# The first weight block of a fused attention and MLP kernel, in two parts, with two layer-1 items interleaved

## The chip, the cores and the metric

The kernel runs on one core of one Trainium2 chip. The metric is the device time of one execution in microseconds (us). Several executions of a kernel are timed and the median is given; one more execution is recorded by the hardware profiler.

## The reference

Causal attention with a decay bias, over 8 batches of 8 heads, 576 positions and a head size of 64, and then a two-layer MLP with exact GELU over the 4608 tokens. `w_in` is 512 x 2048, `w_out` is 2048 x 512, all in float32.

```python
scores = scale * np.matmul(q, k.transpose(0, 1, 3, 2))
cum = np.cumsum(np.maximum(s, 0.0), axis=-1)
bias = -(cum[:, :, :, None] - cum[:, :, None, :])
scores = np.where(causal, -1000000000.0, scores + np.minimum(bias, 0.0))
attn = softmax(scores)                       # rows divided by their sum + 1e-09
x = (attn @ v).transpose(0, 2, 1, 3).reshape(B * S, H * D)
h = x @ w_in
out = (0.5 * h * (1.0 + erf(h / sqrt(2)))) @ w_out
```

## The kernel before

The order of instructions on every engine is written out by hand (a manual schedule). The work has two interleaved streams: attention for a batch of 576 tokens, and the MLP for a chunk of 512 tokens. While chunk `c` goes through the MLP, attention for batch `c + 1` is done between its matmuls. Ahead of the loop stands attention for batch 0 alone.

Attention writes its output, transposed, into `xT`, a ring of 1536 token columns with four rows of blocks (`NP` = 4, 128 values each). For one batch, `av_main(b, 0, ...)` writes rows 0 and 1 for its first 512 tokens, and `av_main(b, 1, ...)` rows 2 and 3. Each consists of the matmuls `av_d` and `av_o` (L459), two pairs of ScalarE activations that form the reciprocal (L474, L475), and four VectorE products into `xT` (L499). The last 64 tokens of a batch are the tails: `av_tails(b, slot)` does 48 small matmuls into one PSUM bank (`av_t`, L459), the reciprocal, and one product (L520). Chunk 0 is tokens 0 to 511, so it does not read batch 0's tails; chunk 1 does.

Layer 1 of a chunk has eight items. An item (`l1_item(c, f2, k0, k1)`, L536) takes 256 columns of `w_in` and consists of 8 matmuls (L546), each over 512 tokens: for each of two groups of 128 columns, one for each of the four rows of `xT`. With `k0, k1 = 0, 2` it does its first half only, the 4 matmuls over rows 0 and 1, and with `k0 = 2` its second half, those over rows 2 and 3. Then one GELU activation (L552, for the last item two at L555) reads the item's two PSUM banks. The pairs of banks are called X, Y and Z, single banks M[0] and M[1]; `order[c]` says in which turn the items of a chunk take X, Y and Z, and later code takes its banks from the same tuple. Layer 2 (`l2_item`, L570, in chunks 0 and 1) multiplies the result with `w_out`.

The weights are loaded by transfers that GpSimd issues (`nc.gpsimd.dma_start`). They stand in its queue behind `behind_v(0, 1)`, a copy that waits for a part of `v` of batch 0. `load_w(0, i)` (L257, L260) loads 1024 columns of `w_in` in four transfers, one for each group of 32 partitions, and changes float32 to bf16 on the way; `load_w(1, i)` (L271) loads a quarter of `w_out` in one. The queue holds them in this order: 8 transfers of `w_in`, 2 of `w_out`, the 4 loads of `q` and `k` for batch 1 (`load_front`, L106), 2 more of `w_out`. Later, SyncE's `behind(1, ...)` (L144) waits for a part of `w_out` and then issues the loads of `v` for batch 1 (`raw_v`, L225), which VectorE scales into `vv` (`scale_v`, L247). VectorE also forms sums of `w_out` (`sums_b`, L598). `squares_v` (L237) is a pass of ScalarE over `raw_v`.

Chunk 0's order on TensorE was: 4 matmuls of item 0 over rows 0 and 1, the tails of batch 0 in bank X, 4 matmuls of item 0 over rows 2 and 3, then items 1 to 7. Chunk 1 already has the other order: first halves of items 0 and 1, tails in M[0], second halves of both.

Of the kernel before, what the change touches and what calls it, by code (L numbers as in the profile page):

```python
# [19 lines left out]
def kernel(  # L20
# [10 lines left out]
    nc = tc.nc  # L31
# [17 lines left out]
    dff = moe_w_in.shape[1]  # L49
    KO = (H * D) // 128  # L50
# [44 lines left out]
    X, Y, Z = "xyz"  # L95
    M = ("m0", "m1")
# [53 lines left out]
    def behind_v(b, st):  # L150

        nc.gpsimd.tensor_copy(seen_v[:, b : b + 1], raws[b, "v"][0:1, st, 0, 0:1])
# [3 lines left out]
    w_in_r = const.tile([128, KO, dff], bf16, name="w_in_r")  # L156
    w_out_r = const.tile([128, FT, KO * 128], fp16, name="w_out_r")
# [84 lines left out]
    def scale_v(b, sts, eng, h0=0, h1=H):  # L242
        t = raws[b, "v"]
        vb = vv[b % 2]
        for st0, st1 in sts:
            n_st = 128 if st1 < ST else SL
            eng.tensor_tensor(  # L247
                vb[:n_st, st0:st1, h0:h1, :],
                t[:n_st, st0:st1, h0:h1, :],
                wb[:n_st, st0:st1, b * H + h0 : b * H + h1]  # L250
                .unsqueeze(3).to_broadcast([n_st, st1 - st0, h1 - h0, D]),
                op=MULT,
            )

    STS = [(st, st + 1) for st in range(ST)]

    def load_w(which, i):  # L257
        if which == 0:
            for g in range(4):
                nc.gpsimd.dma_start(  # L260
                    out=w_in_r[g * 32 : g * 32 + 32, :, i * 1024 : (i + 1) * 1024],
                    in_=bass.AP(
                        tensor=moe_w_in.tensor,
                        offset=moe_w_in.offset + g * 128 * dff + i * 1024,
                        ap=[[dff, 32], [32 * dff, KO], [1, 1024]],
                    ),
                )
        else:
            src = moe_w_out.rearrange("(fo p) m -> p fo m", p=128)[:, i * 4 : (i + 1) * 4, :]
            dst = w_out_r[:, i * 4 : (i + 1) * 4, :]  # L270
            nc.gpsimd.dma_start(out=dst, in_=src)  # L271


    cum, s_pos = s_two
# [147 lines left out]
    def sc_mm(b, p, slots, u0=0):  # L422
        if u0 == 0:
            P_of[b, p] = work.tile([128, 2, PW], bf16, tag="P", bufs=4, name="P")
        P = P_of[b, p]
        for u, slot in enumerate(slots, u0):
            s_ps = bank(slot, [128, 2, 512], fp32, "sc_ps")
            for jt, i0, n, off in UNITS[u]:
                for e in range(2):
                    nc.tensor.matmul(  # L430
                        s_ps[:, e, off : off + n],
                        lhsT=qkT[b % 2][e * 64 : e * 64 + 64, 1, p, jt * 128 : jt * 128 + 128],
                        rhs=qkT[b % 2][e * 64 : e * 64 + 64, 0, p, i0 : i0 + n],
                        start=True, stop=True,
                    )
            nc.scalar.activation(  # L436
                P[:, :, UO[u] : UO[u] + UW[u]], s_ps[:, :, : UW[u]], func=AF.Exp, scale=scale
            )
# [70 lines left out]
    def tails_pe(b, slot):  # L509
        o = bank(slot, [128, 2, 3, SL], fp32, "av_t")  # L510
        for t in (None, 0, 1):
            for qd in range(2):
                av_mm(b, qd, o[:, qd, 0 if t is None else 1 + t], t, TAIL)
        return o

    def tails_out(b, o):
        ln = work.tile([128, 2, SL], fp32, tag="lnt", bufs=1, name="lnt")
        recip(ln, o[:, :, 0], 2)
        for lo, hi, x0 in ring(b, 512, SL):
            nc.vector.tensor_tensor(  # L520
                xT[:, :, x0 : x0 + hi - lo].rearrange("p (a t) x -> p a t x", t=2),
                o[:, :, 1:3, lo:hi],
                ln[:, :, lo:hi].unsqueeze(2).to_broadcast([128, 2, 2, hi - lo]), op=MULT,
            )

    def av_tails(b, slot):
        tails_out(b, tails_pe(b, slot))
# [3 lines left out]

    h_of, o_of = {}, {}

    order = {0: (Y, Z, X)}

    def l1_item(c, f2, k0=0, k1=None):  # L536
        k1 = KO if k1 is None else k1
        if f2 == 0 and k0 == 0:
            gT_of[c] = work.tile([128, FT, NB], fp16, tag="gT", bufs=1, name="gT")
        if k0 == 0:  # L540
            h_of[c, f2] = bank(order[c][f2 % 3], [128, 2, NB], fp32, "h_ps")
        h_ps = h_of[c, f2]
        for i in range(2):
            ft = f2 * 2 + i
            for ko in range(k0, k1):
                nc.tensor.matmul(  # L546
                    h_ps[:, i, :], lhsT=w_in_r[:, ko, ft * 128 : (ft + 1) * 128],
                    rhs=xT[:, ko, c * NB % XW : c * NB % XW + NB],
                    start=(ko == 0), stop=(ko == KO - 1),
                )  # L550
        if k1 == KO and f2 < FT // 2 - 1:
            nc.scalar.activation(gT_of[c][:, f2 * 2 : f2 * 2 + 2, :], h_ps, func=AF.Gelu)  # L552
        elif k1 == KO:
            for i in range(2):
                nc.scalar.activation(gT_of[c][:, f2 * 2 + i, :], h_ps[:, i], func=AF.Gelu)  # L555
# [174 lines left out]
    sc_mm(0, 2, (X, Y))  # L730
    sc_mm(0, 3, (Z, X))
    behind_v(0, 1)
    for i in range(2):
        load_w(0, i)
    for i in range(2):
        load_w(1, i)
    for qd in range(2):
        for n in "qk":
            load_front(1, n, qd)
    for i in range(2, 4):  # L740
        load_w(1, i)
    scale_v(0, STS[0:3], nc.vector)
    mask(0, 2, nc.vector)
    scale_v(0, STS[3:5], nc.vector)
# [3 lines left out]

    for c in range(NCH):
        nb = c + 1  # L750
        if c == 1:
            l1_item(c, 0, 0, KO - 2)
            l1_item(c, 1, 0, KO - 2)
            av_tails(1, M[0])
            l1_item(c, 0, KO - 2)
            l1_item(c, 1, KO - 2)
        else:
            l1_item(c, 0, 0, KO - 2)
            if c == 0:
                av_tails(0, X)  # L760
            l1_item(c, 0, KO - 2)
            l1_item(c, 1)
        if 1 < c and nb < B:
# [168 lines left out]
    with tc.If(rv > 0):  # L932
        with tc.tile_pool(name="gen", bufs=1) as gen, tc.tile_pool(
# [24 lines left out]
            with tc.For_i(0, B, 1) as b:  # L958
# [8 lines left out]
                for h in range(H):  # L967
                    cb = gen.tile([128, S], fp32, tag="cb", bufs=2, name="cb")
                    nc.sync.dma_start(
                        out=cb, in_=c_dram[bass.ds(b * H + h, 1), :].to_broadcast([128, S])  # L970
# [14 lines left out]
                    for it in range(ST):  # L985
# [41 lines left out]
                        g = (h // 2) * 32  # L1027
# [5 lines left out]
            with tc.For_i(0, NCH, 1) as c:  # L1033
                g = gen.tile([128, FT, NB], bf16, name="gg")
# [49 lines left out]
```

## Time and profile before

| | |
|---|---|
| Median of 3 runs | 321.77 us (321.12 to 322.37) |
| Profiled execution, its own time | 320.83 us |
| Span of the profiled execution | 319.0 us |
| TensorE busy | 298.6 us (94%) |
| ScalarE busy | 237.3 us (74%) |
| VectorE busy | 205.2 us (64%) |
| Layer 1 (L546), chain that ended last | 39% of the span |

Times in views of the trace are us from the start of the span. PE is TensorE's matmuls and PEld its weight loads, DVE is VectorE, ACT ScalarE, POOL GpSimd, SP SyncE. A line of the timeline gives start, duration, engine, source line, operation, output and inputs, count, and in brackets the idle time of the engine before it and what ended it. Granted clock (PEclk) is TensorE's clock as a share of full speed.

### The profile page before, as it was taken

How to read it: one execution, taken by the hardware profiler on the slowest of the kernel's cores; microseconds unless marked ns; L12 is line 12 of the kernel's file. 1: busy time of each engine (PE TensorE's matmuls, PEld its weight loads, DVE VectorE, ACT ScalarE, POOL GpSimd, SP SyncE). 2: the span in 40 equal slices, each digit the busy share in tenths (PEclk: the TensorE clock that was granted, in tenths of full speed). 3: DMA queues.
4: the chain of work that ended last, by engine and by line, in shares of the span. 5: the costliest groups of instructions: out<-in, count | busy, mean ns of one | idle time of the engine just before them, and what ended most of it. 6: DMA issues, size and time to landing. Idle time of an engine off the chain costs nothing.

```text
span 319.0 us, 8165 instructions
## 1 busy us (share of the span) xinstructions
PE 298.6 (94%) x3402; PEld 184.1 (58%) x3402; DVE 205.2 (64%) x405; ACT 237.3 (74%) x322; POOL 96.1 (30%) x176
## 2 busy tenths in 40 slices
PE   1769999899999999999999999999999999999991
PEld 0554444544454477647764776477647864784681
DVE  3786317967469758596877487748684875342550
ACT  3775687888965798889887988798779886666510
POOL 6554006205052283409440854076400000000000
PEclk9997999999999999999999999999999999999997
DMA  7999999985913595977699679948890030011003
GB/s 118 205 171 207 206 202 154 273 193 143 189 54 98 99 212 127 257 137 168 132 219 210 147 151 226 207 118 181 190 236 7 2 134 0 2 67 66 2 33 109
DMA packets 77388, 45.05 MB, mean 141 GB/s; under 512 B 63136, under 2 KB 69280, under 8 KB 77344
## 3 DMA queue, kind: packets, MB, share of 16 engines
q1 hardware_dynamic: 67136, 24.93, 33.9%
q0 software_dynamic: 10208, 19.53, 31.7%
q8 instruction: 28, 0.46, 0.6%
q14 instruction: 16, 0.13, 0.2%
HBM read 36.85 MB, written 9.44 MB: 145 GB/s over the span
## 4 chain that ended last, share of the span: by engine, by line
PE 83%; DMA 6%; ACT 5%; DVE 2%; issue 1%; POOL 1%; SPq 0%; ACTq 0%; POOLq 0%
PE h_ps L546 39%; PE o_al L618 16%; PE o_ga L618 8%; PE o_ps L570 5%; PE sc_ps L430 4%; PE o_be L618 4%; PE av_o L459 3%; DMA w_in_r<-in_moe_w_in_dram 3%; PE av_d L459 2%; DMA raw_v<-in_v_dram 2%; ACT junk L237 2%; DMA fq<-in_q_dram 2%; ACT P L436 2%; PE av_t L459 1%; DVE vv L247 1%
## 5 line engine op out<-in xcount | busy, mean ns | idle before, releaser
L546 PE MATMUL h_ps<-xT,w_in_r 128*128 128x512 bf16 x576 | 128.4, 382 | 2.5 <-DMA w_in_r<-in_moe_w_in_dram 2.0
L546 PEld LDWEIGHTS <-w_in_r 128*128 128x128 bf16 x576 | 56.1, 98 | 68.6 <-issue 4.6
L552 ACT ACTIVATE gT<-h_ps 128x1024 f16<-128x1024 f32 x63 | 62.9, 1019 | 26.7 <-PE h_ps L546 26.6
L436 ACT ACTIVATE P<-sc_ps 128x1024 bf16<-128x1024 f32 x64 | 60.3, 1030 | 3.4 <-PE sc_ps L430 3.3
L618 PEld LDWEIGHTS <-S 128*128 128x128 f16 x448 | 42.1, 98 | 6.7 <-issue 0.8
L229 DVE TENSOR_REDUCE amx<-qkT 128x2 f32<-128x1152 bf16 x32 | 41.5, 1344 | 0.1
L609 DVE TENSOR_TENSOR S<-gT 128x1024 f16<-128x1024 f16 x28 | 19.3, 688 | 31.2 <-ACT gT L555 24.0
L618 PEld LDWEIGHTS <-gT 128*128 128x128 f16 x336 | 32.0, 98 | 7.1 <-issue 1.8
L444 DVE TENSOR_TENSOR P<-P,tri_bf 128x512 bf16<-128x512 bf16 x64 | 25.9, 421 | 14.0 <-ACT P L436 13.5
L570 PE MATMUL o_ps<-w_out_r,gT 128*128 128x512 f16 x128 | 30.0, 380 | 0.0
L618 PE MATMUL o_al<-T,S 128*128 128x256 f16 x224 | 27.7, 273 | 0.0
L197 POOL DMA_DIRECT2D raw_k<-in_k_dram x25 | 21.0, 849 | 15.4 <-ACT junk L237 15.4
L430 PE MATMUL sc_ps<-qkT 64*128 64x256 bf16 (+2 forms) x320 | 22.2, 264 | 3.0 <-DVE qkT L400 1.7
L499 DVE TENSOR_TENSOR xT<-av_o,ln 128x256 bf16<-128x256 f32 (+2 forms) x72 | 23.7, 387 | 2.0 <-ACT ln L475 1.1
L247 DVE TENSOR_TENSOR vv<-raw_v,wb 128x512 bf16<-128x512 f32 (+2 forms) x25 | 23.7, 1001 | 0.0
L197 POOL DMA_DIRECT2D raw_q<-in_q_dram x25 | 21.1, 854 | 2.7 <-POOL seen_v L148 2.7
L430 PEld LDWEIGHTS <-qkT 64*128 64x128 bf16 x320 | 13.8, 98 | 12.7 <-issue 7.4
L400 DVE COPY qkT<-tr_ps 128x576 bf16<-128x576 bf16 (+1 forms) x15 | 12.0, 834 | 14.1 <-PE tr_ps L391 14.1
L237 ACT ACTIVATE junk<-raw_v 128x2048 bf16<-128x2048 f32 (+1 forms) x16 | 20.3, 1268 | 0.3
L570 PEld LDWEIGHTS <-gT 128*128 128x128 f16 x128 | 11.5, 98 | 13.6 <-issue 0.7
L475 ACT ACTIVATE ln<-ln,lnb 128x256 f32<-128x256 f32 x32 | 16.3, 508 | 1.0
L459 PEld LDWEIGHTS <-vv 128*32 128x32 bf16 x768 | 16.4, 102 | 0.9 <-issue 0.3
(114 smaller groups left out, 334.4 us busy)
## 6 DMA issues: line engine op xcount, KB each, us to landing
raw_v<-in_v_dram SPq DMA_DIRECT2D x32, 256.0 KB, 4.9
out_dram<-o_sb SPq DMA_DIRECT2D x12, 512.0 KB, 4.3
raw_q<-in_q_dram POOLq DMA_DIRECT2D x20, 256.0 KB, 4.6
raw_k<-in_k_dram POOLq DMA_DIRECT2D x20, 256.0 KB, 6.1
out_dram<-o_sb SPq DMA_DIRECT2D x11, 256.0 KB, 3.6
w_in_r<-in_moe_w_in_dram POOLq DMA_DIRECT2D x8, 256.0 KB, 8.7
w_out_r<-in_moe_w_out_dram POOLq DMA_DIRECT2D x4, 512.0 KB, 13.6
fq<-in_q_dram POOLq DMA_DIRECT2D x6, 288.0 KB, 6.1
```

The source lines that it names most:

```text
L197: nc.gpsimd.dma_start(out=t[:n_st, st], in_=src)
L229: nc.vector.tensor_reduce(amx[:, b * NP + p], qkT[b % 2][:, :, p, :S], axis=AX, op=ALU.max, apply_absolute_value=True)
L237: nc.scalar.activation(n[:n_st, : (st1 - st0) * H * D], t[:n_st, st0:st1].rearrange("p s h d -> p (s h d)"), func=AF.Square, accum_out=amv ...
L247: eng.tensor_tensor(vb[:n_st, st0:st1, h0:h1, :], t[:n_st, st0:st1, h0:h1, :], wb[:n_st, st0:st1, b * H + h0 : b * H + h1] .unsqueeze(3).t ...
L430: nc.tensor.matmul(s_ps[:, e, off : off + n], lhsT=qkT[b % 2][e * 64 : e * 64 + 64, 1, p, jt * 128 : jt * 128 + 128], rhs=qkT[b % 2][e * 6 ...
L436: nc.scalar.activation(P[:, :, UO[u] : UO[u] + UW[u]], s_ps[:, :, : UW[u]], func=AF.Exp, scale=scale)
L444: eng.tensor_tensor(d, d, tri_bf.unsqueeze(1).unsqueeze(1).to_broadcast([128, 2, 2, 128]), op=MULT)
L459: nc.tensor.matmul(o[g * 32 : g * 32 + 32, lo : lo + n], lhsT=(wb[:, jt, b * H + 2 * g + qd : b * H + 2 * g + qd + 1].to_broadcast([128, 3 ...
L546: nc.tensor.matmul(h_ps[:, i, :], lhsT=w_in_r[:, ko, ft * 128 : (ft + 1) * 128], rhs=xT[:, ko, c * NB % XW : c * NB % XW + NB], start=(ko ...
L552: nc.scalar.activation(gT_of[c][:, f2 * 2 : f2 * 2 + 2, :], h_ps, func=AF.Gelu)
L570: nc.tensor.matmul(o_ps, lhsT=gT[:, ft, sub * 128 : (sub + 1) * 128], rhs=w_out_r[:, ft], start=(ft == 0), stop=(ft == FT - 1),)
L618: nc.tensor.matmul(o[u], lhsT=lhs[:, f, u * 128 : u * 128 + 128], rhs=rhs[:, f], start=start and f == 0 and (by_sub or u == 0), stop=f == ...
```

## The change

The first 1024 columns of `w_in` are loaded as two blocks of 512 columns, each in four transfers; the second 1024 columns stay one block of four. That makes 12 transfers instead of 8. Items 0 and 1 read the first block, items 2 and 3 the second, items 4 to 7 the third. Chunk 0's layer 1 takes the order of chunk 1: the first halves of items 0 and 1, the tails in M[0], the second halves of items 0 and 1, then items 2 to 7. `order[0]` becomes X, Y, Z, so item 0 takes X, item 1 takes Y and item 2 takes Z; all later uses of the tuple shift with it.

```diff
-    def load_w(which, i):
-        if which == 0:
-            for g in range(4):
-                nc.gpsimd.dma_start(
-                    out=w_in_r[g * 32 : g * 32 + 32, :, i * 1024 : (i + 1) * 1024],
...
+    def load_w_in(m0, m1):
+        for g in range(4):
+            nc.gpsimd.dma_start(
+                out=w_in_r[g * 32 : g * 32 + 32, :, m0:m1],
+                in_=bass.AP(
+                    tensor=moe_w_in.tensor,
+                    offset=moe_w_in.offset + g * 128 * dff + m0,
+                    ap=[[dff, 32], [32 * dff, KO], [1, m1 - m0]],
+                ),
+            )
...
-    order = {0: (Y, Z, X)}
+    order = {0: (X, Y, Z)}
...
     behind_v(0, 1)
+    for m0, m1 in ((0, 512), (512, 1024), (1024, 2048)):
+        load_w_in(m0, m1)
     for i in range(2):
-        load_w(0, i)
-    for i in range(2):
-        load_w(1, i)
+        load_w_out(i)
...
-        if c == 1:
+        if c < 2:
             l1_item(c, 0, 0, KO - 2)
             l1_item(c, 1, 0, KO - 2)
-            av_tails(1, M[0])
+            av_tails(c, M[0])
             l1_item(c, 0, KO - 2)
             l1_item(c, 1, KO - 2)
         else:
             l1_item(c, 0, 0, KO - 2)
-            if c == 0:
-                av_tails(0, X)
             l1_item(c, 0, KO - 2)
             l1_item(c, 1)
```

More of the change, by code (lines that the diff above doesn't have):

```diff
@@ L255, with load_w_out @@
     STS = [(st, st + 1) for st in range(ST)]
-    def load_w(which, i):
-        if which == 0:
-            for g in range(4):
-                nc.gpsimd.dma_start(
-                    out=w_in_r[g * 32 : g * 32 + 32, :, i * 1024 : (i + 1) * 1024],
[L262 to L271, printed above, removed]
+    def load_w_in(m0, m1):
[8 more added lines that the diff above has]
+            )
+    def load_w_out(i):
+        src = moe_w_out.rearrange("(fo p) m -> p fo m", p=128)[:, i * 4 : (i + 1) * 4, :]
+        nc.gpsimd.dma_start(out=w_out_r[:, i * 4 : (i + 1) * 4, :], in_=src)
     cum, s_pos = s_two
@@ L740 @@
     for i in range(2, 4):
-        load_w(1, i)
+        load_w_out(i)
     scale_v(0, STS[0:3], nc.vector)
```

## The prediction

> **What bounds the kernel now.** I read the page first, then the waits of TensorE (PE), then the chain of waits around the longest of them, and last the windows, the timeline and the DMA view of that place.
>
> ```profile
> PE 298.6 (94%) x3402; PEld 184.1 (58%) x3402; DVE 205.2 (64%) x405; ACT 237.3 (74%) x322; POOL 96.1 (30%) x176
> ```
>
> PE is busy for 94% of the span, so an edit pays only where PE stands still or runs slowly. The waits view of PE from 24 us to 311 us (who waited for whom: us in total, times, longest) says where it stands:
>
> ```profile
> PE h_ps L546 <- DMA w_in_r<-in_moe_w_in_dram: 2.0, 1, 2.0
> PE sc_ps L430 <- ACT P L436: 0.8, 2, 0.5
> PE h_ps L546 <- DVE o_sb L400: 0.5, 1, 0.5
> ```
>
> One wait of 2.0 us is over half of all of it, and the change is aimed at it: the first layer of chunk 0 (L546, the `h_ps` matmuls) waits for the first 1024 columns of `w_in`. The chain of waits (start us, us, what) shows how it ends:
>
> ```profile
> 15.34 8.40 DMA w_in_r<-in_moe_w_in_dram
> 23.75 0.34 issue
> 24.09 1.02 PE h_ps L546 x4
> 25.11 0.74 PE av_t L459 x48
> 25.85 14.41 PE h_ps L546 x60
> ```
>
> The fourth piece of these columns lands at 15.34 + 8.40 = 23.74, and PE takes 0.34 us more to start. What PE and VectorE (DVE) had ready by then, in the timeline:
>
> ```profile
> 17.66 0.82 PE L459 MATMUL av_d<-P,wb 128*32 128x256 bf16 x12 [0.94 <-DVE P L444]
> ...
> 20.60 1.49 PE L459 MATMUL av_o<-P,vv 128*32 128x256 bf16 x30
> 20.19 1.42 DVE L499 TENSOR_TENSOR xT<-av_o,ln 128x256 bf16<-128x256 f32 x4
> 22.19 1.42 DVE L499 TENSOR_TENSOR xT<-av_o,ln 128x256 bf16<-128x256 f32 x4 [0.58 <-PE av_o L459]
> ```
>
> PE stands still up to 17.66 and is through with attention at 20.60 + 1.49 = 22.09. Rows 0 and 1 of `xT`, all that the first halves of layer 1 read, are written at 21.61, rows 2 and 3 at 23.61. So between 22.09 and 24.09 the weights alone are missing.
>
> The gap has a second price. The windows view, cut where the granted clock changes (us; PE busy; PEclk; DMA share; GB/s), and one form of matmul on both sides of it:
>
> ```profile
> 14.87:18.29 3.42, 2.22 (x34) 1.00 0.91 146
> 18.29:21.70 3.41, 3.41 (x80) 1.00 1.04 167
> 21.70:25.11 3.41, 1.40 (x27) 1.00 1.11 205
> 25.11:28.53 3.42, 3.42 (x56) 0.50 1.15 206
> 28.53:40.25 11.72, 11.72 (x55) 1.00 1.23 207
> ...
> L459 PE MATMUL av_o<-P,vv 128*32 128x256 bf16 x48 | 3.4, 407 | 0.0
> ...
> L459 PE MATMUL av_o<-P,vv 128*32 128x256 bf16 x48 | 1.9, 273 | 0.0
> ```
>
> A stretch of 3.41 us in which PE was busy for 1.40 us is followed by one at half clock; a fully busy stretch is followed by full clock. Before 21.70 PE was slow too, though the column reads 1.00 there: the `av_o` matmul takes 407 ns on average between 16 and 22 us and 273 ns between 58 and 62 us. So the stretch to 18.29, 2.22 of 3.42 us busy, did not bring the full clock, and the full one to 21.70 did.
>
> **Part by part. The first block.** Four pieces with 512 columns replace the four with 1024; half the bytes stand ahead of the first matmul. Landings before, for the issues at 13.6 and 14.3 us and for those at 16.9 and 17.5 us, and the packets that finished in three stretches (14 to 20, 20 to 26, 28.6 to 31.5 us):
>
> ```profile
> L260 POOL DMA_DIRECT2D w_in_r<-in_moe_w_in_dram x2: 547/590/632, 13.6 to 14.3; - x2
> ...
> DMA to landing us min/median/max: 4.7/5.8/6.8
> ...
> L260 POOL DMA_DIRECT2D w_in_r<-in_moe_w_in_dram x2: 550/550/550, 16.9 to 17.5; - x2
> ...
> DMA to landing us min/median/max: 10.5/10.8/11.1
> ```
>
> ```profile
> DMA packets 1632, 0.93 MB, mean 155 GB/s; under 512 B 1336, under 2 KB 1336, under 8 KB 1632
> ...
> DMA packets 671, 1.24 MB, mean 206 GB/s; under 512 B 74, under 2 KB 74, under 8 KB 670
> ...
> DMA packets 591, 0.60 MB, mean 208 GB/s; under 512 B 16, under 2 KB 590, under 8 KB 590
> ```
>
> By bytes: the new block is as many as the first two pieces of before, and the second of those landed at 14.3 + 6.8 = 21.1. By packets it is as many (512) as all four pieces of before, which would leave the landing at 23.74. I take the bytes. From 20 to 26 us nearly all are 2 KB packets, about 597 in 6 us, and from 28.6 to 31.5 us 1 KB ones (`w_out`, the shape of the new pieces: 512 floats read, 512 two-byte elements written), 574 in 2.9 us: twice the packets at the same 206 and 208 GB/s. Against it speaks the slow start: 155 GB/s from 14 to 20 us, with only 296 packets of 2 KB, and I can't see why. PE needs the block at 22.09 - 0.34 = 21.75, so 21.1 leaves 0.65 us. The gap of 2.0 us goes. The next stretch is then full, and the half clock of 3.42 us goes with it, which is half of 3.42 us of work: 1.7 us.
>
> **The rule that speaks against the cause of the 1.7 us.** The trace has 1.40 us of work in the stretch before the half clock. The Trainium skill ("TensorE: Matmul & The Clock Gate", What's actually happening) lets the clock fall only after a window of about 3.4 us that is idle. By that rule the 2.0 us gap would not have cost the clock, and the sum would be 2.0 us alone; the row disagrees, since the stretch held work and half clock followed.
>
> **The order of items 0 and 1.** First halves of both (8 matmuls instead of 4), tails, the other halves. The matmuls are the same 64, the tails the same 48; nothing is added on PE. The price of one item at full clock is in the GELU activations, which follow PE:
>
> ```profile
> 25.89 0.28 ACT L474 ACTIVATE lnt<-av_t 128x128 f32<-128x128 f32 x1 [3.29 <-PE av_t L459]
> ...
> 26.62 1.28 ACT L552 ACT_TABLE_LOAD   x1
> 27.91 1.02 ACT L552 ACTIVATE gT<-h_ps 128x1024 f16<-128x1024 f32 x1
> ...
> 31.65 1.02 ACT L552 ACTIVATE gT<-h_ps 128x1024 f16<-128x1024 f32 x1 [0.70 <-PE h_ps L546]
> ...
> 38.55 1.02 ACT L552 ACTIVATE gT<-h_ps 128x1024 f16<-128x1024 f32 x1 [0.70 <-PE h_ps L546]
> ...
> 64.45 0.48 PE av_t L459 x48
> ```
>
> Four items from 31.65 to 38.55 are 1.725 us each; the tails took 0.48 us at full clock in chunk 1. From 22.09: first halves to 23.8 (rows 2 and 3 of `xT` are there at 23.61, as in before), tails to 24.3, other halves to 26.0, item 2 to 27.8, item 3 to 29.5. ScalarE (ACT) needs 2.0 us from the tails' end to the first GELU (25.89 to 27.91), so it starts at 26.4, ends at 27.4 and frees bank X before item 3 wants it at 27.8; cover 0.4 us. The new bank order costs nothing: X was free when ACT had read the last scores, Y is read to 21.61 and Z to 23.61 by the DVE rows above, and the tails' M[0] was read by `av_out`'s first activations.
>
> **The other blocks and the queue.** Block 2 completes the bytes that landed at 23.74 before and is wanted at 26.0. Block 3 completes those of 17.5 + 11.1 = 28.6, wanted at 29.5 less 0.34: cover 0.5 us, nothing if kept, the shortfall itself if not. GpSimd (POOL) issues 12 transfers instead of 8: 4 x 0.55 = 2.2 us more. Behind them stand `w_out` and the loads of batch 1:
>
> ```profile
> POOL w_out_r L271 <- DMA w_in_r<-in_moe_w_in_dram: 3.4, 4, 1.9
> ...
> L271 POOL DMA_DIRECT2D w_out_r<-in_moe_w_out_dram x4: 740/752/762, 18.7 to 28.9; - x4
> ...
> DMA to landing us min/median/max: 12.5/13.6/15.8
> ...
> 49.38 0.69 DVE L598 TENSOR_TENSOR T<-w_out_r 128x1024 f16<-128x1024 f16 x1
> ...
> L225 SPq DMA_DIRECT2D raw_v<-in_v_dram x5: 582/584/2068, 42.7 to 46.1; - x5
> ...
> DMA to landing us min/median/max: 3.3/4.8/5.9
> ...
> 56.70 3.08 DVE L247 TENSOR_TENSOR vv<-raw_v,wb 128x512 bf16<-128x512 f32 x5
> ```
>
> POOL already stands waiting for landings (3.4 us), the first `w_out` leaving at 18.7 as the first piece lands at 13.6 + 4.7 = 18.3; each transfer waits for the one eight before it. So the added issues fall into waits, and the engines keep up to eight transfers to work on. I cost them at nothing. This also means that the loads do not come earlier while PE does, and what is late next must be asked: the last `w_out` lands at 28.9 + 15.8 = 44.7 and is first read by DVE at 49.38, then 45.7: cover 1.0 us. `raw_v` of batch 1 leaves SyncE's queue from 42.7 to 46.1, behind a wait for `w_out`, and is down by 46.1 + 5.9 = 52.0 at the latest; DVE reads it at 56.70, then 53.0: cover 1.0 us again. Without these covers the shortfall stands on DVE ahead of attention's second half, at most the 3.7 us gained.
>
> **The sum.** 2.0 us of gap and 1.7 us of half clock: 3.7 us. The profiled execution took 320.83 us for a span of 319.0 us, so it would take 317.1; the median of the three runs is 321.77, 0.94 us above it, and with the same 3.7 us it becomes 318.1. About 0.5% (1.6 us) is what a measurement of this kernel can tell from no change, so faster means under 320.2.
>
> **The rivals.** *The clock's stretches lie elsewhere.* The stretches are 3.41 us long, and nothing in the trace ties them to the kernel's start. In this profile one ended just before 22.09, so layer 1 can start warm. If the first full one after 17.66 ends later, up to 17.66 + 6.8 = 24.5, the new start runs cold till then and loses up to 1.2 us, and before's loss is 1.7 to 1.9 us as well: the gain is 2.7 us, 319.1. A block 3 that is 1 us late gives the same. I give both together 15%. The same page of the Trainium skill (the same section) calls the window free-running; one profile can't show it.
>
> *Half clock with another cause.* Then only the gap goes: 319.8. The full and the half stretches above speak against it: 5%. The rule of the Trainium skill named above would have it so.
>
> *The first block is bound by packets while the start is slow.* 296 packets are done at 20, the other 216 take 1.1 us at the 1 KB rate (574 in 2.9 us), 21.1 on average; before, 512 packets were reached at 22.2 on average (216 more at 597 in 6 us) and landed at 23.74, so the slowest engine is 1.5 us behind: 22.7, start 23.0. The gain is 1.1 us, with the clock falling as before: 320.7 (319.0 if it stays up). For it: the unexplained 155 GB/s. 12%.
>
> *The gain is lost to the loads.* PE comes to chunk 0's second layer 3.7 us early and waits there for loads that did not move (`raw_v` above first), or packets cost the same whatever their size and all three blocks come late: 321.8, up or down by 1.3. The covers speak against it: 6%.
>
> *Slower: a transfer costs by the piece.* With p us for each of the four added pieces, block 3 lands at 28.6 + 4p. Before, item 2 was done at 31.65, where its GELU began, and item 4 began one item later, at 31.65 + 1.725 = 33.4. It is level at p = 1.1 and 1.6 us worse at p = 1.5. The landings bound p: 18.3 and 21.1 for the first two pieces, 2.8 us apart, which gives 39.8 and 6.7 us lost, 328.5; 1.1 us apart for the last two, and those have twice the bytes. Taken near the middle, p = 2 gives 325.3. 5%, since eight pieces that need up to 11.1 us each land 1.1 us apart and so overlap. The Trainium skill ("DMA: Bandwidth & Descriptors", Anatomy of one DMA) gives each transfer a fixed 2.0 us; were that not overlapped, an estimate by that page is four times 2.0 us and 325.3 us as well.
>
> That PE waits for both blocks all the same is no case of its own: the first weight load of the changed program waits for four transfers, and the load of item 2 for the next four.
>
> **How the numbers follow.** The forecast has 57%: 318.1, within 317.0 and 319.0. With the clock's stretches (15%), the other cause (5%) and the better part of the packets' case the range is 317.0 to 320.3; it leaves out most of that case's 12%, the lost gain, the slower case and some 5% below. Faster: 57 + 15 + 5, and 2 from the packets' case, 79%. Within 0.5%: 10 of the packets' case and 5 of the lost gain, 15%. Slower: 5 and 1, 6%.
>
> **What would show it.** Right: no idle time of PE before the first `h_ps` matmul, which starts by 22.3; no stretch at 0.50 before the end; the last GELU of chunk 0 about 3.7 us earlier; item 2 and item 4 without a wait for `w_in_r`. Wrong: a wait for `w_in_r` before item 0 (the packets' case) or before item 4 (block 3), a stretch at 0.50 without a gap ahead of it, or a wait of PE or DVE for `w_out_r` or `raw_v` between 36 and 60 us.

## The result and the profile after

| | before | changed |
|---|---|---|
| Median of the timed runs | 321.44 us (321.08 to 322.37, 4 runs) | 316.71 us (316.08 to 317.27, 4 runs) |
| Ratio, with its 95% interval | | 0.9848 [0.9818, 0.9877] |
| Profiled execution, its own time | 320.83 us | 316.66 us |
| Span | 319.0 us | 314.8 us |
| PE busy | 298.6 us | 296.7 us |

The change makes the kernel faster by 4.7 us in this comparison, more than the forecast of 3.7 us; the time is 316.71 us where 318.1 us (317.0 to 320.3) was forecast. Runs more than 1.5% above the fastest run of the same kernel beside them (five of the kernel before, none of the changed one) are left out of all ratios and of the counts below. First the page of the changed kernel, PE's line and the share of the chain that ended last:

```profile
PE 296.7 (94%) x3402; PEld 183.6 (58%) x3402; DVE 205.1 (65%) x405; ACT 237.2 (75%) x322; POOL 98.7 (31%) x180
...
PE 85%; ACT 5%; DVE 4%; DMA 2%; issue 1%; POOL 0%; ACTq 0%; POOLq 0%
```

The same 3402 matmuls take 1.9 us less, most of which is the half clock; the rest of the gain is idle time. The waits of PE from 22 to 311 us (who waited for whom: us in total, times, longest):

```profile
PE sc_ps L429 <- ACT P L435: 0.8, 2, 0.5
PE h_ps L545 <- DVE o_sb L399: 0.5, 1, 0.5
PE sc_ps L429 <- ACT qkT L397: 0.2, 1, 0.2
```

The wait of 2.0 us for `w_in` is gone and nothing stands in its place. The chain of waits between 20 and 37 us (start us, us, what) and the GELU activations in the timeline of ScalarE show how layer 1 of chunk 0 now runs:

```profile
20.59 1.15 PE av_o L458 x18
21.74 1.83 PE h_ps L545 x8
23.57 0.48 PE av_t L458 x48
24.05 12.21 PE h_ps L545 x56
```

```profile
26.16 2.85 ACT L551 ACTIVATE gT<-h_ps 128x1024 f16<-128x1024 f32 x3
29.38 1.02 ACT L551 ACTIVATE gT<-h_ps 128x1024 f16<-128x1024 f32 x1 [0.37 <-PE h_ps L545]
...
36.28 1.08 ACT L554 ACTIVATE gT<-h_ps 128x512 f16<-128x512 f32 x2 [0.70 <-PE h_ps L545]
```

PE goes from attention to layer 1 without a pause, and the last GELU starts at 36.28 instead of 40.28 us. The windows (us; PE busy; PEclk; DMA share; GB/s):

```profile
17.83:21.25 3.42, 3.42 (x80) 1.00 1.13 167
21.25:24.66 3.41, 3.41 (x78) 1.00 1.15 198
24.66:28.07 3.41, 3.41 (x17) 1.00 1.11 198
28.07:36.26 8.19, 8.19 (x39) 1.00 1.23 207
```

Every stretch is full, and from 21.25 us on none is at half clock. In the first stretch the column reads 1.00 although PE was still slow: 28 `av_o` matmuls take 1.62 us there, as in the kernel before (30 of them take 1.20 us once the clock is up, in *changed, warm* below). So of the pair of profiles, 4.00 us are won by the end of chunk 0's layer 1: it starts at 21.67 (24.09 before) and takes 14.61 us (16.19 before). At the end the own times are 4.17 us apart.

### The profile page after: what moved, and what is told of

It reads as the page before. It is cut to its first block, busy times and chain, and to the rows that moved or that the text cites. A ratio compares the mean times of both kernels' runs of the same rounds, so it can differ in the third digit from the quotient of the medians.

```text
span 314.8 us, 8169 instructions
## 1 busy us (share of the span) xinstructions
PE 296.7 (94%) x3402; PEld 183.6 (58%) x3402; DVE 205.1 (65%) x405; ACT 237.2 (75%) x322; POOL 98.7 (31%) x180
## 4 chain that ended last, share of the span: by engine, by line
PE 85%; ACT 5%; DVE 4%; DMA 2%; issue 1%; POOL 0%; ACTq 0%; POOLq 0%
PE h_ps L545 39%; PE o_al L617 16%; PE o_ga L617 8%; PE o_ps L569 5%; PE sc_ps L429 5%; PE o_be L617 4%; PE av_o L458 4%; PE av_d L458 2%; DMA fk<-in_k_dram 2%; ACT junk L237 2%; ACT P L435 2%; DVE vv L247 2%; PE av_t L458 1%; PE tr_ps L390 1%; DVE qkT L399 1%
## 5 line engine op out<-in xcount | busy, mean ns | idle before, releaser
L545 PE MATMUL h_ps<-xT,w_in_r 128*128 128x512 bf16 x576 | 127.1, 379 | 0.5 <-DVE o_sb L399 0.5
L197 POOL DMA_DIRECT2D raw_k<-in_k_dram x25 | 21.1, 850 | 13.5 <-DMA raw_v<-in_v_dram 13.5
L197 POOL DMA_DIRECT2D raw_q<-in_q_dram x25 | 21.1, 858 | 0.9 <-POOL seen_v L148 0.6
L458 PE MATMUL av_o<-P,vv 128*32 128x256 bf16 (+1 forms) x512 | 16.8, 273 | 0.0
```

The source lines that it names most:

```text
L197: nc.gpsimd.dma_start(out=t[:n_st, st], in_=src)
L458: nc.tensor.matmul(o[g * 32 : g * 32 + 32, lo : lo + n], lhsT=(wb[:, jt, b * H + 2 * g + qd : b * H + 2 * g + qd + 1].to_broadcast([128, 3 ...
L545: nc.tensor.matmul(h_ps[:, i, :], lhsT=w_in_r[:, ko, ft * 128 : (ft + 1) * 128], rhs=xT[:, ko, c * NB % XW : c * NB % XW + NB], start=(ko ...
```

## The experiments

The theory was the prediction's: the late weights cost the gap, and the gap costs the half clock. Against it stood that the new order matters, that the half clock has another cause, and that the number of transfers costs something. Each kernel was timed beside runs of the kernel before on the same chip. In the table, *L1 end* is the start of the last GELU of chunk 0 and *landing* that of the fourth piece of the first weight block, both from the profiled execution.

| kernel | median us (runs) | ratio to before, 95% | profiled: landing | L1 start | L1 end | own time |
|---|---|---|---|---|---|---|
| before, first profile | 321.77 (3) | | 23.75 | 24.09 | 40.28 | 320.83 |
| changed, first profile | 316.71 (4) | 0.9848 [0.9818, 0.9877] | 19.70 | 21.67 | 36.28 | 316.66 |
| before, repeated | 320.91 (12) | 1.0033 [0.9992, 1.0074] | 22.95 | 23.20 | 37.81 | 319.21 |
| before, p1 to p4 | profiled alone | | 22.58, 22.98, 22.79, 24.86 | 22.83, 23.23, 23.04, 25.11 | 38.85, 39.33, 37.65, 41.33 | 319.49, 320.38, 317.60, 321.86 |
| changed, repeated | 317.38 (12) | 0.9908 [0.9872, 0.9944] | 20.05 | 22.52 | 37.26 | 317.10 |
| changed, third | 316.40 (6) | 0.9879 [0.9823, 0.9934] | 20.29 | 22.26 | 37.14 | 317.39 |
| blocks only | 317.09 (12) | 0.9912 [0.9881, 0.9944] | 19.86 | 22.14 | 36.76 | 317.44 |
| order only | 320.06 (12) | 0.9995 [0.9954, 1.0036] | 23.79 | 24.04 | 40.19 | 320.60 |
| before, gap filled | 318.89 (12) | 0.9986 [0.9952, 1.0020] | 22.92 | 24.08 | 38.68 | 318.53 |
| before, all filled | 318.61 (12) | 0.9968 [0.9930, 1.0006] | 22.94 | 23.19 | 37.80 | 318.49 |
| changed, warm | 316.34 (6) | 0.9893 [0.9843, 0.9943] | 20.09 | 21.06 | 35.77 | 315.89 |
| changed, warm, repeated | 316.21 (6) | 0.9880 [0.9824, 0.9937] | 20.05 | 21.00 | 35.81 | 315.89 |
| changed, warmer | 316.36 (6) | 0.9872 [0.9815, 0.9928] | 21.13 | 21.26 | 37.14 | 317.28 |
| quarters | 318.70 (12) | 0.9974 [0.9935, 1.0012] | | 22.59 | 38.39 | 318.57 |
| sixteen | 316.78 (6) | 0.9880 [0.9823, 0.9936] | | 21.49 | 36.11 | 317.33 |

**Both kernels again.** The changed kernel, and the kernel before as a copy:

> The changed kernel as it is, timed again. Theory A (the gain is the 2.0 us gap and the 1.7 us half clock, and the first comparison's extra 1.0 us came from a stall and an early start that differ from run to run): 3.7 to 4.2 us faster than the kernel before. Theory B (the change brings about 1 us more by something steady that the prediction did not count): 4.6 us or more faster, and a stage behind chunk 0's layer 1 that is shorter in this profile too.

> The kernel before, profiled and timed against itself. Theory A: the attention of batch 0 ends within 0.4 us of 22.09, a half-clock stretch of 3.4 us stands in chunk 0's layer 1, and the 0.35 us stall among the av_t matmuls near 225 us is missing or elsewhere. Theory B: the stall stands at the same place. Times: within 0.3% of itself.

The changed kernel took 317.38 us at a ratio of 0.9908, which is 2.9 us, and the copy 320.91 us. So both theories expected too much gain; the 4.6 us or more of theory B lie outside the interval, the 3.7 to 4.2 us of theory A only in part. All counted runs together: 86 of the kernel before have a median of 320.8 us and reach from 317.41 to 323.26 us; 22 of the changed kernel have a median of 317.0 us and reach from 316.08 to 318.58 us. The difference of the medians is 3.8 us. The kernel before spreads over 5.9 us and the changed one over 2.5 us; the copy's profile shows a part of why, with other stretches than the first profile had, against the expectation of a half-clock stretch in layer 1:

```profile
12.80:16.22 3.42, 1.96 (x58) 1.00 1.12 191
16.22:19.63 3.41, 1.95 (x44) 0.50 1.00 138
19.63:23.04 3.41, 2.71 (x58) 0.50 1.09 202
23.04:26.46 3.42, 3.25 (x61) 1.00 1.13 210
26.46:37.81 11.35, 11.35 (x54) 1.00 1.21 206
```

Here the clock was up by 12.80 us, fell, and was back by 23.04 us, so that layer 1 had no half clock, and its gap was 0.86 us instead of 2.0.

**The blocks alone.** The transfers are split, the old order and the old turn of the banks stay (against the changed kernel):

```diff
-    order = {0: (X, Y, Z)}
+    order = {0: (Y, Z, X)}
...
-        if c < 2:
+        if c == 1:
...
-            av_tails(c, M[0])
+            av_tails(1, M[0])
...
+            if c == 0:
+                av_tails(0, X)
```

> The first 1024 columns in two blocks, but chunk 0's layer 1 in the old order (half of item 0, tails in bank X, other half) and the old banks. Theory A (the early weights alone bring the gain): PE starts layer 1 at about 21.8, then waits 0.1 to 0.3 us for rows 2 and 3 of xT behind the tails; 0.1 to 0.4 us slower than the full change, so 3.4 to 4.0 us faster than before. Rival (the new order is needed, since PE runs out of work without it): 2 us or less faster.

317.09 us, ratio 0.9912: the whole gain. The timeline of PE:

```profile
22.14 1.04 PE L545 MATMUL h_ps<-xT,w_in_r 128*128 128x512 bf16 x4
23.11 0.30 PE L458 MATMUL av_t<-P,wb 128*32 128x64 bf16 x16
23.23 0.43 PE L458 MATMUL av_t<-P,vv 128*32 128x64 bf16 x32
23.60 4.71 PE L545 MATMUL h_ps<-xT,w_in_r 128*128 128x512 bf16 x21
```

No idle time stands in brackets: with 4 matmuls and the tails ahead of it, the second half of item 0 finds rows 2 and 3 of `xT` ready.

**The order alone.** The new order and banks, the first block of 1024 columns whole:

```diff
-    for m0, m1 in ((0, 512), (512, 1024), (1024, 2048)):
+    for m0, m1 in ((0, 1024), (1024, 2048)):
```

> The new order and banks, but the first 1024 columns in one block as before. Theory A: PE waits for w_in_r to about 23.7 to 24.1 as before, half clock follows; within 0.3 us of before. Rival (the order itself brings part of the gain, by more work ahead of the tails): 0.5 to 1.5 us faster.

320.06 us, ratio 0.9995 [0.9954, 1.0036], no gain outside an interval of 1.3 us either way. PE's timeline, and its windows:

```profile
24.04 2.54 PE L545 MATMUL h_ps<-xT,w_in_r 128*128 128x512 bf16 x8 [1.97 <-DMA w_in_r<-in_moe_w_in_dram]
```

```profile
21.73:25.14 3.41, 1.44 (x19) 1.00 1.11 206
25.14:28.55 3.41, 3.41 (x56) 0.50 1.17 205
28.55:40.19 11.64, 11.64 (x55) 1.00 1.23 206
```

Gap and half clock are those of the kernel before. The two parts together say that the earlier weights are all of the effect that these runs can resolve.

**Is the half clock the price of the gap?** In the kernel before, eight matmuls whose result nothing reads are put into the gap; the weights come as they came:

```diff
+    def fill(n, slot):
+        f_ps = bank(slot, [128, NB], fp32, "fill")
+        for i in range(n):
+            nc.tensor.matmul(f_ps, lhsT=ident_bf, rhs=qkT[0][:, 1, 0, 0:NB], start=True, stop=True)
...
+            if c == 0:
+                fill(8, M[0])
             l1_item(c, 0, 0, KO - 2)
```

> The kernel before, with eight matmuls that nobody reads (128x512, bf16) on PE between attention of batch 0 and layer 1 of chunk 0, so that PE stays busy while it would wait for w_in. The weights land as before. Theory A (half clock is the price of the gap): the profile shows no stretch at 0.50 in layer 1 of chunk 0, the median is 1.0 to 1.9 us below the kernel before, and the slowest runs of before (322 to 323) are missing. Rival (half clock has another cause): within 0.4 us of before.

318.89 us. The ratio of 0.9986 [0.9952, 1.0020] does not settle it, as the runs of before beside it had a median of 320.25 us and a spread of 4.9 us; the slowest run with the gap filled took 320.23 us, where those beside it reach 322.35 us. The profile does, PE's timeline (which lacks the record of one of the eight) and windows:

```profile
22.22 2.02 PE L752 MATMUL fill<-qkT,ident_bf 128*128 128x512 bf16 x7
24.08 1.03 PE L546 MATMUL h_ps<-xT,w_in_r 128*128 128x512 bf16 x4
```

```profile
22.50:25.91 3.41, 3.36 (x61) 1.00 1.12 208
25.91:29.32 3.41, 3.36 (x17) 1.00 1.20 208
29.32:38.68 9.36, 9.31 (x44) 1.00 1.22 206
```

Layer 1 starts at 24.08 us, as in the first profile of before (24.09), yet ends at 38.68 instead of 40.28: with the gap busy the clock stays up, and that is worth 1.60 us. So the half clock there is the price of the idle time. The equal start is chance: the weights had landed at 22.92 us in this execution, and the last of the eight matmuls held layer 1 up by 0.9 us more, so the median of this kernel is no price of the clock alone.

**How much is left in the clock?** Four such matmuls ahead of the first `av_main` of batch 0 and between its scores, in the changed kernel and, with the gap's eight, in the kernel before:

```diff
+    fill(2, X)
     sc_mm(0, 2, (X, Y))
...
+    fill(2, M[1])
     av_main(0, 0, M[0], Y)
```

> The changed kernel with four such matmuls more, two ahead of the scores of the third pair of heads and two ahead of attention's sums, where PE stands still for 0.9 us each time. Theory A (what spreads the runs of the changed kernel is when the full clock comes, which needs one busy stretch): the clock is up by 21 us, attention of batch 0 ends up to 0.9 us earlier, and the median is 0.3 to 1.0 us below the changed kernel's 317.4. Rival (the clock comes no earlier, or the fillers stand in the way): 0 to 0.5 us slower.

> The kernel before with all twelve of these matmuls, so that the clock is up on both sides of the gap. What is left between it and the changed kernel with four of them is the late weights alone. Theory A: 2.0 to 2.8 us slower than that one, and 1.5 to 2.5 us faster than before. Rival (the gap costs less than it shows, since later stages wait for loads anyway): less than 1 us slower than that one.

The changed kernel with them took 316.34 us; its clock rose at 14.84 us instead of 21.25, and attention ended at 21.03 instead of 21.74. The kernel before, with all twelve, took 318.61 us, 2.3 us above that: this much the late weights cost beside the clock (in the two profiles layer 1 starts 2.13 us and ends 2.03 us later). A repeat, and one with 13 more at the start:

```diff
+    fill_one(10)
...
+    fill_one(1)
...
+    fill_one(2)
```

> The changed kernel with the four filling matmuls, again, beside the changed kernel on one chip. Theory A: 0.5 to 1.2 us below the changed kernel, with its runs within 1.2 us of each other. Rival (the first comparison of it was luck of the chip): within 0.3 us of it.

> As before, with thirteen more filling matmuls ahead of and among the first transposes, so that the clock is up from about 7 us. Theory A: the transposes and scores of batch 0 run at full clock and attention ends 0.3 to 1.0 us earlier than with four; as much faster. Rival (ScalarE and VectorE set the pace there, or the weights land too late for an earlier start): within 0.3 us of the kernel with four, or a wait for w_in_r of up to 0.5 us.

> The changed kernel again, as the measure on this chip for the three that follow. Theory A (its gain is the gap plus what the clock's stretches make of it, 2 to 4 us from run to run): median 3.0 to 4.2 us below the kernel before.

316.21 and 316.36 us, beside 316.40 us for the changed kernel on the same chip: the warm versions are not measurably better, though two of their profiles show layer 1's end at 35.8 us, and those of the changed kernel between 36.28 and 37.26. The 1.0 us by which the first of them lay below 317.38 us had been measured on another chip. The warmest one waited for the weights again, as its fourth piece landed at 21.13 us in that execution, and a pause in the tails of batch 0, inside layer 1, cost it 1.0 us (waits of PE, then its timeline):

```profile
PE h_ps L545 <- DMA w_in_r<-in_moe_w_in_dram: 0.5, 1, 0.5
```

```profile
24.60 0.24 PE L458 MATMUL av_t<-P,vv 128*32 128x64 bf16 x8 [1.03 <-issue]
```

**What do more transfers cost?** The first 512 columns in two blocks of 256, 16 transfers in all:

```diff
-    for m0, m1 in ((0, 512), (512, 1024), (1024, 2048)):
+    for m0, m1 in ((0, 256), (256, 512), (512, 1024), (1024, 2048)):
```

> The changed kernel with its first block in two more: 256, 256, 512 and 1024 columns, 16 transfers. Theory A (bytes set the landings): layer 1 starts when attention is done, the last block lands within 0.4 us of 28.5, and the time is within 0.5 us of the changed kernel. Rival (a transfer costs by the piece, 1.1 us or more): the last block lands 4 us later, item 4 waits for it, and the time is 3 us or more above the changed kernel.

318.70 us, between the two expectations. The last block came late (PE's timeline), and the DMA view tells when the bytes were lost, with 14 to 20 us and then 20 to 26 us, first of this kernel and then of the changed one:

```profile
31.29 2.97 PE L545 MATMUL h_ps<-xT,w_in_r 128*128 128x512 bf16 x13 [0.85 <-DMA w_in_r<-in_moe_w_in_dram]
```

```profile
DMA packets 2220, 0.79 MB, mean 132 GB/s; under 512 B 1219, under 2 KB 2220, under 8 KB 2220
```

```profile
DMA packets 827, 0.97 MB, mean 162 GB/s; under 512 B 84, under 2 KB 619, under 8 KB 826
```

```profile
DMA packets 1647, 0.91 MB, mean 152 GB/s; under 512 B 973, under 2 KB 1647, under 8 KB 1647
```

```profile
DMA packets 835, 1.17 MB, mean 196 GB/s; under 512 B 94, under 2 KB 444, under 8 KB 834
```

0.32 MB less were moved in these 12 us. A piece of 256 columns writes 64 KB, and GpSimd needs 0.54 us to issue it: 64 KB in 0.54 us are 121 GB/s, below the 206 GB/s of the steady stretches, so the DMA engines could run dry. A piece of 512 columns writes 128 KB, 242 GB/s at the same issue time, and is not bound by it. If that is right, 16 pieces of 128 KB cost nothing. The traces do not show the engines dry, though: their mean busy share is 1.01 in the quarters and 1.04 in the changed kernel from 14 to 20 us, then 1.06 and 1.15, while they move 13% and 17% less. That smaller packets move fewer bytes in the same busy time is the rival, and no run here separates the two. The second half of `w_in` in two blocks:

```diff
-    for m0, m1 in ((0, 512), (512, 1024), (1024, 2048)):
+    for m0, m1 in ((0, 512), (512, 1024), (1024, 1536), (1536, 2048)):
```

> The changed kernel with its last block in two as well: 512, 512, 512 and 512 columns, 16 transfers as in the kernel with quarters, none below 128 KB. Theory A (a transfer costs GpSimd's 0.55 us of issue or its bytes, whichever is longer; 64 KB take less to move than to issue, 128 KB do not): the last block lands within 0.5 us of 28.3, time within 0.5 us of the changed kernel. Rival (each added transfer costs about 0.7 us whatever its size): the last block lands near 31.

316.78 us; the last piece of `w_in` landed at 28.54 us (28.50 in the changed kernel), so the number of transfers is not the cost; both the issue time and the packet's size fit the two runs. The transfers behind were later, though. The issues of `w_out` (duration; first and last start) and their landings, and what VectorE waited for from 40 to 60 us:

```profile
L270 POOL DMA_DIRECT2D w_out_r<-in_moe_w_out_dram x4: 780/801/821, 24.6 to 29.6; - x4
...
DMA to landing us min/median/max: 7.8/12.9/17.1
```

```profile
DVE T L597 <- DMA w_out_r<-in_moe_w_out_dram: 1.5, 1, 1.5
```

The last quarter of `w_out` landed at 29.6 + 17.1 = 46.7 us, and VectorE, which never waited for it in the changed kernel at that place, stood 1.5 us. In that profile the lead at layer 1's end was 4.17 us (36.11 against 40.28), and the own time was only 3.50 us below the first profile of before.

**Four more profiles of the kernel before.** They were to tell what its spread is made of:

> The kernel before, one more profile. Its times go from 317.4 to 323.3 us, and two profiles so far show two placements of the clock's stretches. Theory A (the placement sets the time): with a half-clock stretch behind the gap in layer 1 of chunk 0 the time is 320.3 or more, without one 319.5 or less. Rival (the landing of w_in sets it): the time follows the landing of the fourth piece (22.9 to 23.8 us), whatever the clock does.

> The kernel before, one more profile, as the last: with half clock in layer 1 of chunk 0 320.3 us or more, without it 319.5 or less; by the rival the landing of the fourth piece tells.

> The kernel before, one more profile, as the last two: with half clock in layer 1 of chunk 0 320.3 us or more, without it 319.5 or less; by the rival the landing of the fourth piece tells.

> The kernel before, one more profile, as the last three: with half clock in layer 1 of chunk 0 320.3 us or more, without it 319.5 or less; by the rival the landing of the fourth piece tells.

The fastest, 317.60 us, and the slowest, 321.86 us, by windows and, for the slowest, PE's timeline:

```profile
19.02:22.43 3.41, 3.41 (x74) 1.00 1.10 195
22.43:25.84 3.41, 2.84 (x61) 1.00 1.12 208
25.84:37.65 11.81, 11.81 (x56) 1.00 1.21 206
```

```profile
25.11 1.02 PE L546 MATMUL h_ps<-xT,w_in_r 128*128 128x512 bf16 x4 [2.56 <-DMA w_in_r<-in_moe_w_in_dram]
```

```profile
22.98:26.39 3.41, 1.28 (x48) 1.00 1.11 205
26.39:29.80 3.41, 3.41 (x36) 0.50 1.19 205
29.80:41.33 11.53, 11.53 (x54) 1.00 1.23 207
```

The same kernel loses 0.57 us and no half clock in one execution, 2.56 us and a half stretch in another. Layer 1 starts 0.25 to 0.34 us after the landing in all six profiles of before, and the landing lies between 22.58 and 24.86 us. It takes 14.6 us without half clock and 16.0 to 16.2 us with it (p1, p2, p4, first profile). Neither part alone orders the times: landings from 22.58 to 22.98 go with 317.60 to 320.38 us, and p1, with half clock up to 26.03 us, took 319.49 us. My expectation that half clock always means over 320 us fell with it. The two together do: layer 1's end puts all six profiles in the order of their times, from 37.65 us with 317.60 to 41.33 us with 321.86. The runs without a profile stay open. Six that count, with a mean granted clock of 0.994 to 0.998, took over 320.9 us, where others at the same clock took 317.41 us; since the clock's record can read 1.00 while PE is slow, it does not tell what they lost. From layer 1's end to the end of the execution all kernels of the table take 279.8 to 281.4 us; in the profiles of before most of what differs there is a pause in `av_t` that the waits put down to "issue" (none to 1.0 us).

## Why the prediction was right or wrong

**The step that failed is the last of the sum: putting the gain on the median of three runs.** The profile's own time less 3.7 us was 317.1 us, and that is where the changed kernel is: 316.66, 317.10 and 317.39 us in three profiles, 317.0 us for the median of 22 runs. I added the 0.94 us by which the median lay above the profile, as if the changed kernel carried it too, and set the range's end at 317.0. That is 0.94 of the 1.4 us missed; most of the rest is that the two profiles came out 4.17 and not 3.7 us apart, of which 0.35 us, the earlier end of attention, was luck of that execution (21.74 us; 22.59 and 22.33 in the other two profiles). The 0.94 us is not a constant of the measurement. One execution of before that is 1 us above the first profile has its weights land later: p4 is 1.03 us above it (321.86 against 320.83), its layer 1 started 1.02 us and ended 1.05 us later. This is the very wait that the change takes away, so the changed kernel has no share in it. The three timed runs were not profiled, so that their 0.94 us was this wait too is argued from p4 and not shown. (They were also high: 321.77 us, where 86 runs have 320.8.) The mechanism, that the split removes a loss which differs from run to run, was in the prediction only as a rival about the clock.

**The gap (2.0 us).** Right for that profile, and shown by the blocks alone. It was sized from one execution: six have 0.57 to 2.56 us. In the profile pair layer 1 started 2.42 us earlier; attention itself ended 0.35 us earlier, as PE came to it at 17.42 instead of 17.66 us and the clock rose at 21.25 instead of 21.70.

**The half clock (1.7 us).** Right in kind, shown by the filled gap (1.60 us), and 1.58 us in the profile pair. It too is there in some executions of before only: four of six. In two of the four, p1 and p2, the clock had fallen at 15.79 and 16.35 us, ahead of the gap; that the gap kept it down there is not shown. Stretches with 1.28, 1.40 and 1.96 us of work in 3.41 were followed by half clock, one with 2.84 us by full clock. The rule of the Trainium skill weighed in the prediction ("TensorE: Matmul & The Clock Gate", What's actually happening), by which the clock falls only after an idle window, does not hold in these rows; that the borders of the windows run free of the kernel, as the same section has it, agrees with them. The rival that the half clock has another cause falls for the profile that was priced.

**The first block.** It landed at 19.70 us, earlier than either bound (21.1 and 23.74), and it was there 1.7 us before PE needed it (at 21.67 less 0.25 us). The issues (duration; first and last start) and landings:

```profile
L259 POOL DMA_DIRECT2D w_in_r<-in_moe_w_in_dram x12: 545/545/634, 13.5 to 20.0; - x12
...
DMA to landing us min/median/max: 4.3/5.8/8.5
```

So neither bytes ahead of it nor packets, as I counted them, set it. The cover, estimated at 0.65 us, was 1.7 us, and the packets' rival falls; what set the landing stays open.

**Items 2 to 7 and the last block.** Item 3 done at 29.38 (forecast 29.5); the last block at 20.0 + 8.5 = 28.5 (28.6), with no wait. The added issues did cost nothing at 128 KB a piece; the quarters show that the step holds for that size and not at 64 KB. That is the truth in the rival of a price by the piece: not a price per transfer, but one of small pieces, by their issue time or by their packets. The fixed 2.0 us that the Trainium skill ("DMA: Bandwidth & Descriptors", Anatomy of one DMA) gives each transfer is not seen in the sum: 16 transfers of `w_in` were down at 28.54 us and 12 at 28.50.

**The covers behind.** The timeline of VectorE:

```profile
45.38 0.69 DVE L597 TENSOR_TENSOR T<-w_out_r 128x1024 f16<-128x1024 f16 x1
...
52.70 3.09 DVE L247 TENSOR_TENSOR vv<-raw_v,wb 128x512 bf16<-128x512 f32 x5
```

Read at 45.38 and 52.70 us (forecast 45.7 and 53.0), without a wait. `w_out` landed at 28.8 + 15.8 = 44.6 us, so 0.8 us of the 1.0 us of cover was left; where it landed 2.1 us later, in the run of sixteen, VectorE waited. The cover was as thin as forecast.

**The order.** Costed at nothing, and worth nothing that these runs can resolve.

## What to carry to other kernels

The wait that one profile shows can be a quantity that differs between executions: before adding a gain to a median, profile the kernel several times, and don't hand on to the changed kernel the part of the spread that comes from the wait removed. When TensorE waits for the first weights, a smaller first block pays twice, since an idle stretch can cost the clock afterwards; fill the gap with work nobody reads to learn which share is the clock's. Compare a piece's bytes with its issue time before splitting further (here 128 KB a piece cost nothing and 64 KB did), and look at what stands behind it in the queue.

## What the runs showed of the hardware that I had not expected

- **How much work keeps or raises the clock.** The granted clock changes at borders 3.41 us apart that lie elsewhere in each execution. A stretch at full clock with 1.28 (p4), 1.40 (first profile) or 1.96 us of work (copy of before) was followed by half clock; one with 2.84 us (p3) was not. Upwards, a stretch with 2.71 us (copy of before) was followed by full clock, those with 2.52 us (p2) and 2.72 us (p1) by half clock, so the busy time of this view alone does not decide it. The windows of p2, then of p1, whose first stretch here is the one in which the clock had fallen:

```profile
19.76:23.18 3.42, 2.52 (x54) 0.50 1.11 205
23.18:26.59 3.41, 3.36 (x54) 0.50 1.12 207
```

```profile
15.79:19.20 3.41, 2.14 (x48) 0.50 1.03 166
19.20:22.61 3.41, 2.72 (x54) 0.50 1.08 198
22.61:26.03 3.42, 3.20 (x54) 0.50 1.11 206
```

- **The wait's name can mislead.** In three profiles of before the waits put PE's stand ahead of layer 1 (0.9 to 1.0 us) down to VectorE's `xT`, which was then still writing rows 2 and 3; but PE started 0.25 us after the landing in these as in p3 and p4, where the wait bears the weights' name.
- **The pauses "issue" in `av_t`**, 0.2 to 1.0 us once in an execution and in some executions none, are as large as the differences that the warm versions were to show. Five of the six profiles of before have one, always at the same place, in the tails at 222 to 226 us behind 13 of the 32 matmuls with `vv`; the three profiles of the changed kernel have none. They average 0.4 us over the six, so a part of what the changed kernel gains may be theirs and not the weights': the mean own times of these profiles are 2.8 us apart, the mean ends of layer 1 2.3 us. What makes them stays open.
- **Why the DMA engines move only 152 GB/s from 14 to 20 us** stays open too. In these 6 us of the changed kernel 899 packets of about 250 bytes, of another queue than GpSimd's, took 19.2% of the 16 engines' time for 0.22 of the 0.91 MB; from 20 to 26 us, at 196 GB/s, there were none.
